# First MLP block: half-columns of 128 tokens for its first three columns, among the small products of chunk 1

## The chip, the cores and the metric

One core of a Trainium2 chip runs the program. TensorE (PE) multiplies, VectorE (DVE), ScalarE (ACT) and GpSimd (POOL) do the elementwise work, SyncE (SP) and ACT issue most DMAs. Each engine works through its own instructions in the order in which the program has them, and waits at semaphores for the others. The metric is the device time of one execution in microseconds, lower is better.

## The reference

A delta-rule attention over 768 steps, then two MLPs on its output, all in float32.

```python
# attention: q, k, v are (4, 8, 768, 48), beta is (4, 8, 768)
k_n = k / (norm(k) + 1e-06)
for t in range(S):
    y[:, :, t] = einsum('bhd,bhde->bhe', q[:, :, t], state)
    v_old = einsum('bhde,bhd->bhe', state, kt)
    state = state + bt * einsum('bhd,bhe->bhde', kt, vt - v_old)
x = y.transpose(0, 2, 1, 3).reshape(3072, 384)
# first MLP: d_ff 2048
h = x @ w_in
x = (maximum(h, 0) + alpha * minimum(h, 0)) @ w_out
# second MLP: d_ff 1536
g = x @ w_gate
out = (g * sigmoid(g) * (x @ w_val)) @ w_out2
```

## The kernel before

The 768 steps are cut into 24 chunks of 32; a chunk holds 4 batches x 32 steps = 128 tokens. Four chunks form a window. In a chunk c the recurrence is done with small products: KS (keys times state, `do_KS`, tile pk), QS (queries times state, py), U (the triangular inverse TT times v, tile pu), S (the state's update, pst), Y (py again, masked weights times U, copied to ys by ACT) and XT (PE transposes ys to px, ACT takes its rounded part as xh, DVE the rest as xl). Each small product is 32 matmuls, two instructions for each on PE. Chunk 0 has no state; for chunk 1, KS and QS are products with chunk 0's U, and S(1) does both chunks at once (128 instructions). The triangular inverse of a window comes from `lanes2` (window 0, with the products pi on PE) or `lanes` (the others: DVE and POOL eliminate row by row; it begins with two transposes into L on DVE and is called the solve below). `pre_T` (pt) transposes keys and queries of a window, `pre_G` (pg) makes their products, which ACT copies to GL and mt.

The first MLP works in blocks n of two chunks, 256 tokens, and 16 columns j of 128 hidden units. `H1(n, j)` is nine matmuls with 256 moving columns (three slices of 128 inputs, for each: high part times high, high times low, low times high), then ACT's Relu into pn and DVE's sum for the PReLU. `H1_parts` splits pn into gh: ACT rounds, POOL subtracts. `O1(n, j)` is nine matmuls more, whose last three need POOL's part; they add to the block's output in PSUM.

The weights of the first MLP arrive as 64-bit floats and are converted on the chip, one column at a time, by the generator `all_w1`, of which `go(conv)` does a step: three steps a column. The first has ACT's scaling of the next column's words, DVE's first pass, ACT's rounding of the column before (L887) and POOL's subtraction for it (L875, two halves); the second and third are DVE's second and third pass (L599, L603) and, from column 4 on, the loads of later columns, issued by ACT. Sixteen steps are in the prelude, the other 33 in the main loop's first eleven columns.

The order is written by hand. `prelude` (L913) is a straight list of calls. What follows it is a list of events, each with a due time in units of a column, sorted by it: H1(0, j) is due at j, its parts at j + 0.45, O1 at j + 2.5; chunk 2 and 3 get theirs from `base(c)`; the solve of window 1 has 37 steps between 10.9 and 22.6. The due times set only the order in which each engine gets its instructions.

The PSUM tiles of H1 rotate over two buffers, pn and gh over three each.

Of the kernel before, what the change touches and what calls it, by code (L numbers as in the profile page):

```python
# [24 lines left out]
def kernel(  # L25
# [646 lines left out]

    g1_t, o1_t = {}, {}

    def H1(n, j):
        ps = ps_h1.tile([128, 512], F32, name="h1", tag="h1")
        w = w1[j][:, 0]
        x = x1_t[n]
        i = 0
        for kk in range(NK):  # L680
            for a, b in PASSES:
                nc.tensor.matmul(  # L682
                    ps[:, 0:N1],
                    w[:, a, kk * 128:kk * 128 + 128],
                    x[b][:, kk, :],
                    start=(i == 0),
                    stop=(i == 3 * NK - 1),
                )
# [7 lines left out]
        g1_t[n, j] = g  # L696

    def H1_parts(n, j):
        g = g1_t[n, j]
        gh = g1.tile([128, 2, N1], F32R, name="gh", tag="gh", bufs=3)  # L700
# [313 lines left out]
    for w in range(1, NWIN):  # L1014
        P = base(4 * w) - 32
        if w == 1:
            for z in range(2):
                at(1.4 + 1.2 * z, lambda: go(inv0[0]))
            for z in range(4):
                at(1.8 + 1.05 * z, pre_T, 1, "q", z // 2, z % 2, nat)  # L1020
            for z in range(4):
                at((5.7, 7.0, 8.8, 10.4)[z], lambda z=z: pre_G(4 + z, raw=True))
                at(13.0 + 2 * z, mask_m, 4 + z)
            for z in range(2):
                at((4.3, 6.4)[z], lambda z=z: pre_G(2 + z, (1,), raw=True))
# [27 lines left out]
        for z in range(n):  # L1053
            at(l0 + (l1 - l0) * z / n, step)

    at(0.5, do_S, 1)
    at(0.6, load_k2, 2)
    for c in range(2, NCH):
        u = base(c)
        f = {2: 0.8, 3: 0.8, 4: 0.6, 5: 0.6}.get(c, 1.0)  # L1060
        if c > 2:
            at(u - 7, load_v, c)
            at(u - 1.3, load_k2, c)
        at(u - 1.5, scale_v, c)
        at(u + 0.3, do_KS, c)
        at(u + 0.35, do_QS, c)
        at(u + 0.3 + 2 * f, do_U, c)
        at(u + 0.3 + 4 * f, do_S, c)
        at(u + 0.3 + 5 * f, do_Y, c)
        at(u + 0.3 + (7 if c < 4 else 6) * f, do_XT, c)  # L1070
# [81 lines left out]
```

## Time and profile before

| | us |
|---|---|
| median of 3 runs | 1093.32 (1093.03 to 1093.74) |
| the profiled execution | 1094.43 |
| its span | 1092.5 |
| PE busy | 1055.2 (97%) |
| DVE busy | 603.6 (55%) |
| ACT busy | 389.9 (36%) |
| POOL busy | 359.5 (33%) |

The shares are means over very different stretches: the attention and the first MLP overlap in the first part, and the second MLP, almost all PE, fills the end. Times in the trace are counted from the span's start. A matmul's busy time includes the time it takes to run out behind the next one, so the distance from one start to the next is what a matmul costs in a row of them.

### The profile page before, as it was taken

The numbers are of one execution on the slowest core, as the hardware profiler recorded it, in microseconds if no ns is written. First come the engines' busy times: TensorE is split into PE (matmuls) and PEld (weight loads), VectorE is DVE, ScalarE is ACT, GpSimd is POOL, SyncE is SP. The second block draws the span as 40 slices with busy tenths as digits, with TensorE's granted clock in tenths as the row PEclk, the third lists the DMA queues.
The fourth block names the chain that finished last, engine by engine and source line by source line (L and its number), as shares of the span: only waits on it lengthen the run. The fifth ranks groups of instructions, "written<-read, shape, count | busy, mean of one in ns | idle before, by whom it ended". The sixth has DMA issues, their size and how long they took to land.

```text
span 1092.5 us, 35673 instructions
## 1 busy us (share of the span) xinstructions
PE 1055.2 (97%) x15649; PEld 969.6 (89%) x15649; DVE 603.6 (55%) x1204; ACT 389.9 (36%) x841; POOL 359.5 (33%) x531
## 2 busy tenths in 40 slices
PE   6689899999999999999999999999999999999998
PEld 5588788999999999999999998888888888888887
DVE  5778865975895697489453453433333333333332
ACT  3556343343434334433444653222222222222211
POOL 3478852832563383366333541101001001010000
PEclk9669999999999999999999999999999999999999
DMA  9663042353344236330441541010010010100001
GB/s 196 184 192 105 10 103 53 62 122 95 70 69 134 66 62 139 90 82 11 118 130 56 159 135 54 1 58 1 1 58 1 18 42 1 58 1 1 29 1 29
DMA packets 165979, 76.34 MB, mean 70 GB/s; under 512 B 129824, under 2 KB 160576, under 8 KB 165824
## 3 DMA queue, kind: packets, MB, share of 16 engines
q1 hardware_dynamic: 160256, 66.28, 24.5%
q10 hardware_dynamic: 5184, 7.37, 2.2%
q8 instruction: 122, 2.00, 0.8%
q0 software_dynamic: 384, 0.41, 0.2%
q14 instruction: 33, 0.27, 0.1%
HBM read 57.52 MB, written 16.52 MB: 68 GB/s over the span
## 4 chain that ended last, share of the span: by engine, by line
PE 89%; POOL 4%; issue 2%; DVE 2%; DMA 1%; ACT 1%; SPq 0%; ACTq 0%; POOLq 0%; DVEq 0%
PE gv L772 27%; PE o L713 18%; PE h L682 18%; PE o L802 14%; PE pst L527 2%; PE pg L207 2%; PE pu L506 2%; PE py L548 2%; PE pk L462 2%; PE py L462 1%; POOL w L875 1%; DMA nat<-in_k_dram 1%; POOL gh L702 1%; POOL X L331 1%; POOL tmg L323 1%
## 5 line engine op out<-in xcount | busy, mean ns | idle before, releaser
L772 PE MATMUL gv<-x2s,w 128*128 128x512 f32 x1296 | 307.6, 391 | 0.0
L772 PEld LDWEIGHTS gv<-x2s,w 128*128 128x128 f32 x1296 | 242.5, 188 | 47.8
L713 PE MATMUL o<-gh,w 128*128 128x256 f32 x1728 | 246.2, 288 | 3.9 <-POOL gh L702 3.9
L682 PE MATMUL h<-xh,w 128*128 128x256 f32 x1152 | 241.2, 286 | 3.0 <-DVE pn L693 1.6
L702 POOL TENSOR_TENSOR gh<-pn,gh 128x256 fp32r<-128x256 f32 x192 | 155.3, 809 | 248.5 <-ACT gh L701 217.3
L713 PEld LDWEIGHTS o<-gh,w 128*128 128x128 f32 x1728 | 217.3, 189 | 11.5 <-POOL gh L702 5.1
L682 PEld LDWEIGHTS h<-xh,w 128*128 128x128 f32 x1152 | 192.2, 191 | 5.8 <-DVE pn L693 2.6
L693 DVE SCALAR_TENSOR_TENSOR pn<-pn,slope,h 128x256 f32<-128x256 f32 x192 | 91.3, 476 | 135.9 <-ACT pn L692 135.9
L682 PE MATMUL h<-xl,w 128*128 128x256 f32 x576 | 163.2, 283 | 0.1
L802 PE MATMUL o<-w,us 128*128 128x384 f32 x864 | 162.5, 337 | 0.0
L802 PEld LDWEIGHTS o<-w,us 128*128 128x128 f32 x864 | 151.9, 188 | 7.1 <-DVE os L815 1.4
L692 ACT ACTIVATE pn<-h,slope 128x256 f32<-128x256 f32 x192 | 90.4, 471 | 137.7 <-PE h L682 134.5
L784 DVE TENSOR_TENSOR sg<-sg,gv 128x512 f32<-128x512 f32 x72 | 49.5, 687 | 151.8 <-ACT sg L782 151.7
L701 ACT ACTIVATE gh<-pn 128x256 fp32r<-128x256 f32 x192 | 80.0, 417 | 145.0 <-DVE pn L693 143.2
L682 PEld LDWEIGHTS h<-xl,w 128*128 128x128 f32 x576 | 109.8, 191 | 0.6 <-DVE xl L574 0.6
L757 POOL TENSOR_TENSOR x2s<-x2r,x2s 128x512 fp32r<-128x512 f32 x15 | 19.3, 1320 | 266.6 <-ACT x2s L755 266.6
L789 ACT ACTIVATE us<-u 128x512 fp32r<-128x512 f32 x72 | 45.5, 632 | 171.2 <-DVE u L785 171.2
L782 ACT ACTIVATE sg<-gv 128x512 f32<-128x512 f32 x72 | 43.0, 597 | 159.3 <-PE gv L772 159.3
L790 DVE TENSOR_TENSOR us<-u,us 128x512 fp32r<-128x512 f32 x72 | 49.9, 693 | 54.8 <-ACT us L789 54.8
L785 DVE TENSOR_TENSOR u<-sg,gv 128x512 f32<-128x512 f32 x72 | 49.5, 688 | 49.3 <-PE gv L772 48.8
L331 DVE TENSOR_TENSOR X<-X,tmp 128x31 f32<-128x31 f32 (+29 forms) x155 | 65.0, 419 | 4.8
L323 DVE TENSOR_TENSOR tmp<-L,X 128x31 f32<-128x31 f32 (+29 forms) x155 | 59.5, 384 | 1.8
(120 smaller groups left out, 975.9 us busy)
## 6 DMA issues: line engine op xcount, KB each, us to landing
w<-in_moe_w_out_dram SPq DMA_DIRECT2D x19, 384.0 KB
wf<-w2d SPq DMA_DIRECT2D x36, 192.0 KB
k<-in_k_dram SPq DMA_DIRECT2D x96, 48.0 KB
x2d<-xs SPq DMA_DIRECT2D x12, 384.0 KB
w<-in_moe_w_gate_dram SPq DMA_DIRECT2D x12, 384.0 KB
w<-in_moe_w_val_dram SPq DMA_DIRECT2D x12, 384.0 KB
x2r<-x2d SPq DMA_DIRECT2D x24, 192.0 KB
v<-in_v_dram SPq DMA_DIRECT2D x88, 48.0 KB
```

Source lines behind the costliest of these rows:

```text
L323: eng.tensor_tensor(w, t.L[:, i + 1:C, i:i + 1].to_broadcast([128, n, m]), t.X[:, i:i + 1, c0:c0 + m].to_broadcast([128, n, m]), ALU.mult,)
L331: eng.tensor_tensor(Xv, Xv, w, ALU.subtract)
L682: nc.tensor.matmul(ps[:, 0:N1], w[:, a, kk * 128:kk * 128 + 128], x[b][:, kk, :], start=(i == 0), stop=(i == 3 * NK - 1),)
L692: nc.scalar.activation(out=g, in_=hv, func=AF.Relu, scale=slope[:, 0, j:j + 1])
L693: nc.vector.scalar_tensor_tensor(out=g, in0=g, scalar=slope[:, 1, j:j + 1], in1=hv, op0=ALU.mult, op1=ALU.add)
L701: nc.scalar.activation(out=gh[:, 0], in_=g, func=AF.Copy)
L702: nc.gpsimd.tensor_tensor(gh[:, 1], g, gh[:, 0], ALU.subtract)
L713: nc.tensor.matmul(o[:, dm // 2, (dm % 2) * N1:(dm % 2) * N1 + N1], w[:, a, dm * 128:dm * 128 + 128], g[:, b], start=(j == 0 and i == 0 an ...
L772: nc.tensor.matmul(p[:, 0:N2], w2[j, z][:, a, kk * 128:kk * 128 + 128], x[:, b, kk], start=(i == 0), stop=(i == 3 * NK - 1),)
L784: nc.vector.tensor_tensor(sg, sg, ps[0], ALU.mult)
L790: nc.vector.tensor_tensor(us[:, 1], u, us[:, 0], ALU.subtract)
L802: nc.tensor.matmul(o2_t[n][t][:, 0:DM], us[:, a, t * 128:t * 128 + 128], w[:, b, :], start=(j == 0 and i == 0), stop=(j == J2 - 1 and i == 2),
```

## The change

In the prelude, chunk 0's QS and Y come before KS(1), and XT(0) right behind KS(1). Behind it QS(1), U(1) and Y(1) of chunk 1 follow, and between them and XT(1) stand the first halves (tokens 0 to 127, which are chunk 0's) of H1 and of the split for the columns 0, 1 and 2; the first half of O1 of column 0 closes the prelude. The second halves (tokens 128 to 255) of these three columns and their other halves of O1 are events of the main loop. H1, H1_parts and O1 get the token range as arguments; a half has nine matmuls as a whole has, with 128 moving columns.

The due times around the first eleven columns are other ones: S(1) goes from 0.5 to 2.6, KS and QS of a chunk no longer stand next to each other, and the pre_T, pre_G and mask events of window 1 and the last steps of window 0's inverse move.

```diff
-    def H1(n, j):
+    def H1(n, j, c0=0, c1=N1):
         ps = ps_h1.tile([128, 512], F32, name="h1", tag="h1")
...
+        hv = ps[:, c0:c1]
         for kk in range(NK):
             for a, b in PASSES:
                 nc.tensor.matmul(
-                    ps[:, 0:N1],
+                    hv,
                     w[:, a, kk * 128:kk * 128 + 128],
-                    x[b][:, kk, :],
+                    x[b][:, kk, c0:c1],
...
-    def O1(n, j):
-        if j == 0:
+    def O1(n, j, c0=0, c1=N1):
+        if j == 0 and c0 == 0:
...
-                    o[:, dm // 2, (dm % 2) * N1:(dm % 2) * N1 + N1],
+                    o[:, dm // 2, (dm % 2) * N1 + c0:(dm % 2) * N1 + c1],
                     w[:, a, dm * 128:dm * 128 + 128],
-                    g[:, b],
+                    g[:, b, c0:c1],
...
         do_U(0)
         go(conv, C_C)
-        do_KS(1)
         do_QS(0)
         do_Y(0)
+        do_KS(1)
         mark(nat[0][0:1, 0, 0, 0:1])
         load_nat(1, "q", nat)
         load_v(2)
         go(conv, 2)
-        do_U(1)
-        do_QS(1)
-        go(conv, 3)
         do_XT(0)
...
-        go(conv, C_D)
+        do_QS(1)
+        do_U(1)
+        go(conv, 1)
+        H1(0, 0, 0, 128)
+        go(conv, 1)
+        H1_parts(0, 0, 0, 128)
         do_Y(1)
         go(conv, 1)
+        H1(0, 1, 0, 128)
+        go(conv, C_D)
+        H1_parts(0, 1, 0, 128)
         do_XT(1)
+        go(conv, 1)
+        H1(0, 2, 0, 128)
+        H1_parts(0, 2, 0, 128)
+        O1(0, 0, 0, 128)
...
-        return {2: 2.9, 3: 7.7, 4: 22.6, 5: 27.2}.get(c, 8 * (c - 2))
+        return {2: 3.4, 3: 7.8, 4: 22.6, 5: 27.2}.get(c, 8 * (c - 2))
...
-                at((5.7, 7.0, 8.8, 10.4)[z], lambda z=z: pre_G(4 + z, raw=True))
+                at(6.6 + z, lambda z=z: pre_G(4 + z, raw=True))
...
+    FIRST = {2: (3.6, 4.6, 5.1, 6.1, 7.1, 8.15), 3: (8.1, 9.1, 10.1, 11.1, 12.1, 12.8)}
+    at(2.6, do_S, 1)
+    at(2.7, load_k2, 2)
...
     for n in range(NB1):
         for j in range(J1):
+            if n == 0 and j < 3:
+                at(0.7 * j, H1, n, j, 128, N1)
+                at(0.7 * j + 0.3, H1_parts, n, j, 128, N1)
+                if j > 0:
+                    at(0.7 * j, O1, n, j, 0, 128)
+                at(2.1 + 0.01 * j if j < 1 else 2.5 + j, O1, n, j, 128, N1)
+                continue
```

On PE, from U(0) to the first column of the MLP, before (pu is U, pk is KS, py is QS or Y, px is XT, h is H1; mx and mt are the weights of the products with chunk 0's U and of the masked ones):

```order
L506 MATMUL pu<-v,TT 32x48 x32
L475 MATMUL pk<-U,mx 32x48 x32
L548 MATMUL py<-U,mt 32x48 x32
L506 MATMUL pu<-v,TT 32x48 x32
L475 MATMUL py<-U,mx 32x48 x32
L570 MATMUL px<-ident,ys 128x128 x3
L548 MATMUL py<-U,mt 32x48 x32
L570 MATMUL px<-ident,ys 128x128 x3
L682 MATMUL h_1025<-xh,w 128x256
```

and of the change, from the same U(0), where h_965 is the first half of column 0:

```order
L506 MATMUL pu<-v,TT 32x48 x32
L548 MATMUL py<-U,mt 32x48 x32
L475 MATMUL pk<-U,mx 32x48 x32
L570 MATMUL px<-ident,ys 128x128 x3
L475 MATMUL py<-U,mx 32x48 x32
L506 MATMUL pu<-v,TT 32x48 x32
L683 MATMUL h_965<-xh,w 128x128
L683 MATMUL h_965<-xl,w 128x128
L683 MATMUL h_965<-xh,w 128x128 x2
L683 MATMUL h_965<-xl,w 128x128
L683 MATMUL h_965<-xh,w 128x128 x2
L683 MATMUL h_965<-xl,w 128x128
```

Chunk 0's transposes (px) stand two products earlier, and the nine matmuls of a half-column follow chunk 1's U; behind them come Y(1), nine more of column 1, XT(1), and nine more of column 2.

On POOL, in the same place and the main loop's first columns, before (w is a converted weight's low part, two instructions, named by its words w_113 of column 3 and so on; gh is a column's split, v the scaling of a chunk's v):

```order
L875 TENSOR_TENSOR w<-w_113,w 128x384 x2
L875 TENSOR_TENSOR w<-w_114,w 128x384 x2
L875 TENSOR_TENSOR w<-w_115,w 128x384 x2
L702 TENSOR_TENSOR gh<-pn,gh 128x256
L875 TENSOR_TENSOR w<-w_116,w 128x384 x2
L452 TENSOR_TENSOR v<-v,nn 128x384
L702 TENSOR_TENSOR gh<-pn,gh 128x256
L875 TENSOR_TENSOR w<-w_117,w 128x384 x2
L702 TENSOR_TENSOR gh<-pn,gh 128x256
```

and of the change:

```order
L883 TENSOR_TENSOR w<-w_113,w 128x384 x2
L707 TENSOR_TENSOR gh<-pn,gh 128x128 x2
L883 TENSOR_TENSOR w<-w_114,w 128x384 x2
L707 TENSOR_TENSOR gh<-pn,gh 128x128
L883 TENSOR_TENSOR w<-w_115,w 128x384 x2
L707 TENSOR_TENSOR gh<-pn,gh 128x128 x2
L883 TENSOR_TENSOR w<-w_116,w 128x384 x2
L707 TENSOR_TENSOR gh<-pn,gh 128x128
L452 TENSOR_TENSOR v<-v,nn 128x384
L883 TENSOR_TENSOR w<-w_117,w 128x384 x2
```

Two of the split's halves now stand ahead of the weights of column 4, three ahead of those of column 5, and all six ahead of those of column 7, where before one whole split stood ahead of column 6's.

On PE, about column 7 of the main loop, before (o is O1, pk and py here are KS and QS of chunk 3):

```order
L548 MATMUL py<-U,mt 32x48 x32
L713 MATMUL o_1253<-gh,w 128x256 x9
L462 MATMUL pk<-St,kqt 32x48 x32
L682 MATMUL h_1880<-xh,w 128x256
L682 MATMUL h_1880<-xl,w 128x256
L682 MATMUL h_1880<-xh,w 128x256 x2
L682 MATMUL h_1880<-xl,w 128x256
L682 MATMUL h_1880<-xh,w 128x256 x2
L682 MATMUL h_1880<-xl,w 128x256
L682 MATMUL h_1880<-xh,w 128x256
L462 MATMUL py<-St,kqt 32x48 x32
L713 MATMUL o_1253<-gh,w 128x256 x9
```

and of the change, from the same Y(2):

```order
L548 MATMUL py<-U,mt 32x48 x32
L721 MATMUL o_1069<-gh,w 128x256 x9
L207 MATMUL pg<-kqt 32x64 x32
L683 MATMUL h_1879<-xh,w 128x256
L683 MATMUL h_1879<-xl,w 128x256
L683 MATMUL h_1879<-xh,w 128x256 x2
L683 MATMUL h_1879<-xl,w 128x256
L683 MATMUL h_1879<-xh,w 128x256 x2
L683 MATMUL h_1879<-xl,w 128x256
L683 MATMUL h_1879<-xh,w 128x256
L462 MATMUL pk<-St,kqt 32x48 x32
L570 MATMUL px<-ident,ys 128x128 x3
```

Chunk 3's KS stands a column's H1 later there, with a pre_G in its place, and its QS a further column later.

## Rows read from the trace of the kernel before

**Rows 1.** Busy time by stretch: us, then each engine, clock, DMA share, GB/s.

```profile
40.00:50.00 10.00, 6.56 (x299) 5.69 (x291) 6.98 (x8) 6.18 (x10) 3.85 (x4) 0.59 0.44 109
...
130.00:140.00 10.00, 6.85 (x53) 6.02 (x51) 9.42 (x20) 3.15 (x9) 9.14 (x19) 1.00 0.08 30
...
160.00:180.00 20.00, 20.00 (x614) 18.44 (x607) 8.45 (x19) 7.62 (x20) 4.93 (x6) 1.00 0.26 72
```

**Rows 2.** Waits of PE, 36 to 150 us: total, times, longest.

```profile
PE o L713 <- POOL gh L702: 3.9, 6, 1.8
PE py L548 <- issue: 2.0, 1, 2.0
...
PE pk L462 <- issue: 2.0, 1, 2.0
...
PE pg L207 <- issue: 1.2, 1, 1.2
```

**Rows 3.** Timeline of PE before column 0: start, length, operation, wait before.

```profile
51.76 1.01 PE L548 MATMUL py<-U,mt 32*32 32x48 f32 x36 [2.00 <-issue]
53.41 0.90 PE L570 MATMUL px<-ident,ys 128*128 128x128 f32 x3 [0.64 <-ACT ys L557]
55.68 0.58 PE L682 MATMUL h<-xh,w 128*128 128x256 f32 x1 [1.37 <-ACT xh L573]
```

**Rows 4.** Busy time in stretches of 2 us; the clock is third from last.

```profile
50.00:52.00 2.00, 0.24 (x13) 0.24 (x16) 1.37 (x3) 0.57 (x2) 2.00 (x3) 0.91 1.15 259
...
66.00:68.00 2.00, 2.00 (x10) 2.00 (x11) 1.93 (x4) 2.00 (x6) 0.65 (x1) 0.50 0.88 244
...
70.00:72.00 2.00, 2.00 (x136) 1.97 (x136) 1.97 (x2) 1.81 (x4) 2.00 (x3) 1.00 0.82 243
...
76.00:78.00 2.00, 2.00 (x67) 1.88 (x58) 1.88 (x2) 0.00 (x0) 2.00 (x3) 0.50 1.09 341
```

**Rows 5.** Chain of waits, 0 to 200 us: start, length, what.

```profile
58.35 3.60 PE pst L527 x128
61.95 2.22 PE h L682 x9
...
79.77 1.06 PE h L682 x9
```

**Rows 6.** Weight loads of PE by shape: busy us, mean ns.

```profile
L682 PEld LDWEIGHTS h<-xh,w 128*128 128x128 f32 x1152 | 192.2, 191 | 5.8 <-DVE pn L693 2.6 <-ACT xh L573 1.8
...
L527 PEld LDWEIGHTS pst<-U,k 32*64 32x64 f32 x1472 | 25.0, 140 | 2.9 <-issue 0.4
L506 PEld LDWEIGHTS pu<-v,TT 32*32 32x32 f32 x1536 | 19.3, 109 | 4.4 <-issue 0.8 <-POOL w L875 0.7
```

**Rows 7.** Timeline of PE in the second MLP, with 512 moving columns.

```profile
904.58 4.29 PE L772 MATMUL gv<-x2s,w 128*128 128x512 f32 x18
908.71 2.25 PE L802 MATMUL o<-w,us 128*128 128x384 f32 x12
```

**Rows 8.** Timeline of DVE, chunk 1's xl to the solve's first transpose.

```profile
55.66 0.56 DVE L574 TENSOR_TENSOR xl<-px,xh 128x384 fp32r<-128x384 f32 x1 [0.88 <-ACT xh L573]
...
57.20 1.66 DVE L603 SCALAR_TENSOR_TENSOR w<-w 128x768 int32<-128x768 int32 x1
...
62.01 0.56 DVE L540 COPY St<-pst 128x384 f32<-128x384 f32 x1 [1.16 <-PE pst L527]
...
65.64 0.48 DVE L693 SCALAR_TENSOR_TENSOR pn<-pn,slope,h 128x256 f32<-128x256 f32 x1 [2.12 <-ACT pn L692]
...
73.46 0.47 DVE L693 SCALAR_TENSOR_TENSOR pn<-pn,slope,h 128x256 f32<-128x256 f32 x1
...
112.87 1.11 DVE L269 STREAM_TRANSPOSE L<-GL 128x512 f32<-128x512 f32 x1 [1.74 <-ACT GL L217]
```

**Rows 9.** Waits of DVE, 50 to 150 us.

```profile
DVE pn L693 <- ACT pn L692: 6.2, 6, 2.1
DVE xl L574 <- ACT xh L573: 3.2, 3, 1.7
```

More of the change, by code (lines that the diff above doesn't have):

```diff
@@ L689, in H1 @@
                 i += 1
-        hv = ps[:, 0:N1]
-        g = g1.tile([128, N1], F32, name="pn", tag="pn", bufs=3)
+        if c0 == 0:
+            g1_t[n, j] = g1.tile([128, N1], F32, name="pn", tag="pn", bufs=3)
+        g = g1_t[n, j][:, c0:c1]
         nc.scalar.activation(out=g, in_=hv, func=AF.Relu, scale=slope[:, 0, j:j + 1])
@@ L695, in H1, with H1_parts @@
         )
[L696 to L700, printed above, removed]
+    gh_t = {}
+    def H1_parts(n, j, c0=0, c1=N1):
+        g = g1_t[n, j][:, c0:c1]
+        if c0 == 0:
+            gh_t[n, j] = g1.tile([128, 2, N1], F32R, name="gh", tag="gh", bufs=3)
+        gh = gh_t[n, j][:, :, c0:c1]
         nc.scalar.activation(out=gh[:, 0], in_=g, func=AF.Copy)
         nc.gpsimd.tensor_tensor(gh[:, 1], g, gh[:, 0], ALU.subtract)
-        g1_t[n, j] = gh
-    def O1(n, j):
-        if j == 0:
+        if c1 == N1:
+            g1_t.pop((n, j))
+    def O1(n, j, c0=0, c1=N1):
+        if j == 0 and c0 == 0:
             o1_t[n] = ps_o1.tile([128, 2, 512], F32, name="o1", tag="o1")
@@ L709, in O1 @@
         w = w1[j][:, 1]
-        g = g1_t.pop((n, j))
+        g = gh_t[n, j]
+        if c1 == N1:
+            gh_t.pop((n, j))
         for i, (a, b) in enumerate(((0, 0), (1, 0), (0, 1))):
@@ L713, in O1 @@
                 nc.tensor.matmul(
-                    o[:, dm // 2, (dm % 2) * N1:(dm % 2) * N1 + N1],
+                    o[:, dm // 2, (dm % 2) * N1 + c0:(dm % 2) * N1 + c1],
                     w[:, a, dm * 128:dm * 128 + 128],
-                    g[:, b],
-                    start=(j == 0 and i == 0 and dm % 2 == 0),
+                    g[:, b, c0:c1],
+                    start=(j == 0 and i == 0 and dm % 2 == 0 and c0 == 0),
                     stop=(j == J1 - 1 and i == 2),
@@ L1017 @@
             for z in range(2):
-                at(1.4 + 1.2 * z, lambda: go(inv0[0]))
+                at(3.1 + z, lambda: go(inv0[0]))
             for z in range(4):
-                at(1.8 + 1.05 * z, pre_T, 1, "q", z // 2, z % 2, nat)
+                at((3.7, 4.7, 5.15, 5.65)[z], pre_T, 1, "q", z // 2, z % 2, nat)
             for z in range(4):
-                at((5.7, 7.0, 8.8, 10.4)[z], lambda z=z: pre_G(4 + z, raw=True))
+                at(6.6 + z, lambda z=z: pre_G(4 + z, raw=True))
                 at(13.0 + 2 * z, mask_m, 4 + z)
             for z in range(2):
-                at((4.3, 6.4)[z], lambda z=z: pre_G(2 + z, (1,), raw=True))
-                at((4.9, 7.5)[z], mask_m, 2 + z)
+                at((5.6, 10.6)[z], lambda z=z: pre_G(2 + z, (1,), raw=True))
+                at((6.3, 11.2)[z], mask_m, 2 + z)
             l0, l1, n = 10.9, 22.6, LANES
@@ L1054 @@
             at(l0 + (l1 - l0) * z / n, step)
-    at(0.5, do_S, 1)
-    at(0.6, load_k2, 2)
+    FIRST = {2: (3.6, 4.6, 5.1, 6.1, 7.1, 8.15), 3: (8.1, 9.1, 10.1, 11.1, 12.1, 12.8)}
+    at(2.6, do_S, 1)
+    at(2.7, load_k2, 2)
     for c in range(2, NCH):
         u = base(c)
-        f = {2: 0.8, 3: 0.8, 4: 0.6, 5: 0.6}.get(c, 1.0)
+        f = {4: 0.6, 5: 0.6}.get(c, 1.0)
         if c > 2:
@@ L1064 @@
         at(u - 1.5, scale_v, c)
[L1065 to L1070, printed above, removed]
+        cols = [u + 0.3 + z * f for z in (0, 0.05, 2, 4, 5, 6)]
+        for x, fn in zip(FIRST.get(c, cols), (do_KS, do_QS, do_U, do_S, do_Y, do_XT)):
+            at(x, fn, c)
     for n in range(NB1):
         for j in range(J1):
+            if n == 0 and j < 3:
[5 more added lines that the diff above has]
+                continue
             at(16 * n + j, H1, n, j)
```

## The prediction

> **What bounds the kernel now.** I read the busy share by stretch first, then the waits of TensorE (PE), then PE's own timeline where it waits, then the clock, and last the engine that is late next.
>
> The stretches [rows 1] show three regimes. From 160 us PE is busy 20.00 of 20 us: what comes later is a fixed quantity of matmuls, and whatever is won or lost before moves the end by the same amount. Between 40 and 50 us PE is busy 6.56 of 10 us, because chunk 1's small products hang on each other. Between 130 and 140 us it is busy 6.85 of 10 while VectorE (DVE) has 9.42 and GpSimd (POOL) 9.14: there the triangular solve of window 1 sets the pace. The change works before that stage and on the way to it.
>
> From 36 to 150 us PE's waits [rows 2] are of two kinds. Waits for "issue" (the largest 2.0, 2.0 and 1.2 us) are stops in which no engine is late; waits for POOL's gh (3.9 us) belong to the solve. Between 56 and 112 us PE waits for no other engine, so its own work is the bound there, while ScalarE (ACT), DVE and POOL convert the weights in the same rhythm, interleaved with the columns in program order.
>
> The timeline of PE before the first MLP column [rows 3] shows the holes: 2.00 us in the middle of chunk 1's last product, 0.64 us before its transposes, 1.37 us before column 0. The granted clock [rows 4] is 0.91 at 50 to 52 us, 0.50 from 52 us, still 0.50 at 66 to 68 us, and 1.00 at 70 to 72 us; there is a second fall, 0.50 at 76 to 78 us, behind the 2.0 us stop in KS. At 0.50 (1.2 GHz) the nine matmuls of a column's first product take 2.22 us, at 1.00 (2.4 GHz) 1.06 us [rows 5].
>
> **The change part by part.** The sum is made at one place, the start of the solve of window 1 (its L transposes, 112.87 us [rows 8]), against the profiled execution of 1094.43 us (span 1092.5 us and 1.9 us around it). That one is 1.1 us above the median of 1093.32 us.
>
> Order of chunk 0 and 1 before the MLP. Product Y(0) now stands before KS(1), and XT(0) before U(1). U(1) becomes later by the length of Y(0) less what it waited for; Y(1) then ends near 53.0 us as before (52.8 us, [rows 3]), because the 2.00 us stop comes at a place counted in instructions and shrinks as the work before it gets longer. I take 0 for this reordering, with -1 and +1.5 us as ends (half the stop gained, or one half-column of 9 matmuls at the low clock between Y(1) and XT(1) lying on the chain). On the queues of ACT and DVE the same sixteen conversion steps are issued in this part; SP's loads keep their order except that v of chunk 3 now goes ahead of k of chunk 2, both long before their use, which I cost at nothing: PE has some ten columns' work to cover them.
>
> More matmuls. Three columns of 18 matmuls with 256 moving columns become six half-columns of 18 with 128. Behind chunk 1's transposes PE has 54 such matmuls before; now 90 of the half size (36 of H1 and 54 of O1; of these 18 before the main loop, the rest in it). The price of a half-size one isn't in the trace. Low end: from 512 columns (18 in 4.13 us, 229 ns each [rows 7]) to 256 (1.06/9 = 118 ns [rows 5]) a matmul loses 0.43 ns per column, which makes 62 ns for 128. High end: 118 ns, no saving at all, because each of them still needs its own 128 weight columns loaded: the loads take 109, 140 and 191 ns for 32, 64 and 128 columns [rows 6], 0.85 ns per column or 109 ns for the 128, about what 256 moving columns take. A load can hide behind one matmul before it, and behind 128 columns only half of it fits. I take 118 ns: 36 x 0.118 = +4.2 us. The low end gives 90 x 0.062 - 54 x 0.118 = -0.8 us; at 2.22/9 = 247 ns (low clock) it is +8.9 us.
>
> The Trainium skill, "TensorE: Matmul & The Clock Gate", section "LDWEIGHTS (loading the stationary operand)", says that a load's time is its columns over 1.2 in ns, whatever the rows: 107 ns for 128. This speaks against halving, and the slope of the three load rows agrees with it. By that rule the term would be 90 x 0.107 - 6.4 = +3.3 us. The same page, "Back-to-back issue gap", gives about 81 ns for 128 columns sustained, by which it would be +0.9 us; no run here shows it yet.
>
> Clock. Before, PE ran at 0.50 from about 55.7 to 68.7 us, 13 us for work that takes 6.2 at 1.00: 6.8 us. What preceded the fall was the 2.00 us stop and the holes behind it. Now nine matmuls stand before Y(1), nine between Y(1) and XT(1), nine behind it, so that PE hardly stops between 48 us (when the clock had risen) and the main loop. I take it that the clock stays up: -6.8 us; ends 0 and -8.6 us (with the second fall, 3.5 us x 0.52 = 1.8 us, of which I take half, -0.9).
>
> Stops for issue behind 56 us. 2.0 and 1.2 us [rows 2] come where groups of 64 small matmuls are adjacent (KS next to QS, pg next to S and pg). The new order puts one group between the 9 matmuls of H1 and those of O1 in more places. The number of instructions isn't lower, so I take half: -1.6 us of 3.2 (ends 0 and -3.2).
>
> PE alone: 4.2 - 6.8 - 0.9 - 1.6 = -5.1 us.
>
> **What is late next.** DVE. From the end of chunk 1's xl (55.66 + 0.56 us) to column 3's pn at 73.46 us [rows 8] it has 17.2 us, of which 1.16 + 2.12 = 3.3 us are waits; in that stretch it then has four half-size pn instead of three whole ones (0.47 us each), which I count as 0.5 us more. So column 3 can come 2.8 us earlier at most, however fast PE is. The rest must come in the columns 4 to 10, where DVE waits too: all its waits for PE by way of ACT sum to 6.2 + 3.2 + 1.7 us [rows 8, 9], so the far end for the whole stage is -11 us. The last GL now comes from pre_G at 9.6 instead of 10.4, which takes away DVE's 1.74 us wait at 112.87 us. Of the 2.3 us left of PE's gain I believe half, 1.2 us: -4.0 us in all. The solve stage and all behind it are shifted whole, since POOL and DVE (solve) and then PE (to the end) have the same work. 1094.43 - 4.0 = 1090.4 us for a profiled execution, 1089.3 us as a median.
>
> **Rivals.**
> 1. Halves at the low clock (slower). If the clock falls all the same at 52 us and stays at 0.50 as it did before, the nine groups behind Y(1) (H1 of columns 1 and 2, O1 of 0, three second H1, two first O1 halves and the second of column 0) take 1.92 us each by the full price (2.22 less 0.3 us, the end of the last matmul, which the next group covers). From 53.0 us this reaches 71 us, and S(1) (3.60 us for its 128 small matmuls [rows 5]) 74.6 us. Before, column 3 had its pn at 73.46 us, some 2 us behind the start of its H1, so it begins 3 us later; the pi products and transposes that were done by then are still to come (+2), less 2 us of stops: +3 us, 1096.3 us. It decides from the point where column 3 begins after 73.5 us. For it: from 56 to 68 us PE worked without a hole and stayed at 0.50. Against: the holes ahead of the fall are shorter.
> 2. The conversion hides it. ACT, DVE and POOL go through the weights one per column in either kernel, and of these DVE's third pass alone takes 1.66 us at 57.20 us [rows 8]. If DVE holds 5.2 us per column, PE's gain turns into waits for pn: within 1.5 us of before, 1092.5 us.
> 3. The halves are cheap (62 ns), the clock stays up and the stops go: -0.8 - 8.6 - 3.2 = -12.6 us for PE, cut by DVE to about -8: 1085.3 us.
>
> **How the numbers follow.** Main case 0.42 (1087.5 to 1091.3 us); rival 1 0.17; rival 2 0.25; rival 3 0.16. Faster or slower by 0.2% means 2.2 us, about what a measurement of this kernel tells from no change. Faster: 0.39 + 0.03 + 0.16 = 0.58; slower: 0.15 + 0.01 = 0.16; same: 0.26. The range leaves out half of rival 3's far side and half of rival 1's: 1084.8 to 1095.8 us.
>
> **What would show it.** Right: granted clock 1.00 from 54 to 70 us; column 3's pn between 70 and 72 us; L transposes near 109 us; 9 half-size matmuls in about 1.0 us. Wrong: clock 0.50 in that stretch and column 3 after 73.5 us (rival 1); DVE without waits and PE waiting for pn, L transposes near 112 us (rival 2); 9 halves in under 0.7 us (rival 3).

## The result: slower by 1.1%, and the profile after

| | before | after |
|---|---|---|
| median of 6 runs each, same chip, us | 1094.21 (1093.03 to 1096.12) | 1105.88 (1101.99 to 1109.58) |
| ratio, 95% interval | | 1.0107 [1.0085, 1.0128] |
| profiled execution: span, mean granted clock | 1092.5, 0.984 | 1104.0, 0.966 |

The forecast was 1089.3 us, between 1084.8 and 1095.8, with a chance of 0.16 for slower. The change costs 11.7 us, and the range does not hold it.

The stretches that answer to [rows 1] (us; busy time of PE, PEld, DVE, ACT, POOL; clock, DMA share, GB/s):

```profile
40.00:50.00 10.00, 7.93 (x318) 6.92 (x309) 5.98 (x9) 4.93 (x9) 4.69 (x4) 0.55 0.57 136
130.00:140.00 10.00, 8.79 (x71) 8.25 (x70) 9.62 (x29) 2.68 (x7) 9.06 (x21) 1.00 0.12 22
160.00:180.00 20.00, 19.48 (x549) 18.33 (x537) 9.47 (x22) 9.36 (x26) 5.79 (x8) 1.00 0.30 78
```

PE's holes from 40 to 50 us did shrink (7.93 of 10 us busy, before 6.56). From 160 to 180 us PE is full but for 0.52 us (19.48, before 20.00). Most of the loss lies between.

The clock comes next. These are stretches of 2 us of the changed kernel, with the same columns, as in [rows 4].

```profile
54.00:56.00 2.00, 2.00 (x21) 1.88 (x11) 0.00 (x0) 0.49 (x1) 1.58 (x3) 0.50 0.44 83
...
66.00:68.00 2.00, 2.00 (x11) 2.00 (x11) 1.94 (x2) 1.59 (x2) 2.00 (x2) 0.50 0.79 239
70.00:72.00 2.00, 2.00 (x11) 2.00 (x10) 1.97 (x2) 0.68 (x1) 2.00 (x2) 0.50 0.94 320
...
76.00:78.00 2.00, 2.00 (x9) 1.81 (x9) 1.37 (x2) 0.49 (x1) 0.24 (x1) 0.50 0.69 160
84.00:86.00 2.00, 2.00 (x11) 2.00 (x10) 1.61 (x2) 0.66 (x2) 0.80 (x2) 0.50 0.31 40
```

The clock falls in the same place as before, but where it was back at 70 to 72 us [rows 4] it is now at 0.50 in every stretch up to 86 us, although PE is full in each of them. The trace also records when the granted clock changes. By these records the low stretches behind 50 us are 52.5 to 86.6 and 90.1 to 93.5 us; before they were 51.7 to 68.7 and 75.5 to 79.0: 20.5 us have become 37.5.

PE's timeline there (start, length, operation, wait before) shows the halves:

```profile
50.73 0.44 PE L548 MATMUL py<-U,mt 32*32 32x48 f32 x19
53.09 1.18 PE L548 MATMUL py<-U,mt 32*32 32x48 f32 x45 [1.93 <-issue]
54.20 0.48 PE L683 MATMUL h<-xh,w 128*128 128x128 f32 x1
...
58.65 2.12 PE L721 MATMUL o<-gh,w 128*128 128x128 f32 x9
60.57 0.41 PE L683 MATMUL h<-xh,w 128*128 128x128 f32 x1
...
72.22 3.67 PE L527 MATMUL pst<-U,k 32*64 32x48 f32 x128
75.82 0.58 PE L683 MATMUL h<-xh,w 128*128 128x256 f32 x1
...
84.18 0.56 PE L683 MATMUL h<-xh,w 128*128 128x256 f32 x1
```

Nine half-size matmuls of O1 take from 58.65 to 60.57 us, 0.213 us each. The long row of half-size matmuls ends at 72.22 us, where S(1) begins, and column 3's H1, of whole size, starts at 75.82 us. So the clock stays low through half-size matmuls first, and then through S(1), columns 3 and 4, nine more halves of O1 and the small products between them.

The stop in Y(1) is still there, 1.93 us against 2.00 [rows 3], but at another place in it: behind the 19th of its 64 matmul instructions, where before it stood behind the 28th:

```profile
49.23 0.53 PE L548 MATMUL py<-U,mt 32*32 32x48 f32 x28
```

The nine half-size matmuls that now stand ahead of Y(1) have moved it forward by nine. Counted along PE's matmul instructions such stops come at fixed distances. Before, 128 and 127 matmuls lie between the stops that end at 43.69, 47.07 and 51.76 us, and 511 more up to the one at 75.32 us; in the change 255 lie between those at 44.01 and 53.09 us, and 638 more up to the one at 90.11 us. Each is a multiple of 128, less two at most; not every multiple shows a stop.

The waits of PE from 36 to 150 us (total, times, longest), to be held against [rows 2]:

```profile
PE py L548 <- issue: 3.3, 2, 1.9
PE o L721 <- POOL gh L707: 2.9, 2, 1.8
PE pi L430 <- issue: 2.3, 1, 2.3
PE py L548 <- POOL mt L195: 1.9, 1, 1.9
PE py L462 <- issue: 0.8, 1, 0.8
```

Of the kernel before, this view also has two stops that stand before 44 us:

```profile
PE pk L475 <- issue: 2.0, 1, 2.0
...
PE pi L430 <- issue: 2.0, 1, 2.0
```

In all, the waits for issue sum to 10.8 us before and to 6.4 us now; behind 56 us they sum to 4.2 us (2.0, 1.2, 0.6 and 0.4) and to 0.8 us. So they have become fewer. One wait is new: Y(2) for its mask on POOL, 1.9 us.

DVE's timeline, as in [rows 8], and its waits from 50 to 150 us, as in [rows 9]:

```profile
78.71 0.48 DVE L695 SCALAR_TENSOR_TENSOR pn<-pn,slope,h 128x256 f32<-128x256 f32 x1 [1.34 <-ACT pn L694]
...
120.14 1.12 DVE L269 STREAM_TRANSPOSE L<-GL 128x512 f32<-128x512 f32 x1
123.46 0.48 DVE L695 SCALAR_TENSOR_TENSOR pn<-pn,slope,h 128x256 f32<-128x256 f32 x1 [2.20 <-ACT pn L694]
...
124.89 1.13 DVE L269 STREAM_TRANSPOSE L<-GL 128x512 f32<-128x512 f32 x1
```

```profile
DVE pn L695 <- ACT pn L694: 16.5, 10, 3.5
```

Column 3's pn is 5.25 us late (78.71 against 73.46) and the first L transpose 7.27 us (120.14 against 112.87). DVE waits 16.5 us for pn by way of ACT, before 6.2. The wait for GL is gone, but between the two transposes DVE now waits 2.20 us for a column's pn. The second transpose is therefore 9.67 us late; before it stood here:

```profile
115.22 1.08 DVE L269 STREAM_TRANSPOSE L<-GL 128x512 f32<-128x512 f32 x1
```

The end is 11.5 us late. The rest is lost about 182 us, where PE has a stop for issue of 1.95 us (up to 181.43 us), and behind it the clock is low from 182.2 to 185.6 us (a stretch of 4 us):

```profile
182.00:186.00 4.00, 4.00 (x77) 3.60 (x76) 0.64 (x2) 1.05 (x3) 0.00 (x0) 0.57 0.01 4
```

A column's pn ahead of it is 9.48 us late (176.40 against 166.92 us), one behind it 11.76 us (205.52 against 193.76). Another short low stretch, from 144.7 to 148.1 us, falls into the solve and costs at most 0.4 us: the pn on either side are 9.17 and 9.49 us late (137.75 against 128.58, 152.80 against 143.31). The kernel before has neither low stretch.

### The profile page after: what moved, and what is told of

It is laid out like the page before. It is cut to its first block, busy times and chain, and to the rows that moved or that the text cites. A ratio compares the mean times of both kernels' runs of the same rounds, so it can differ in the third digit from the quotient of the medians.

```text
span 1104.0 us, 35796 instructions
## 1 busy us (share of the span) xinstructions
PE 1070.3 (97%) x15703; PEld 986.3 (89%) x15703; DVE 604.1 (55%) x1207; ACT 391.9 (36%) x847; POOL 358.1 (32%) x534
## 4 chain that ended last, share of the span: by engine, by line
PE 91%; POOL 3%; issue 2%; DMA 2%; DVE 1%; SPq 1%; ACT 0%; ACTq 0%; POOLq 0%; DVEq 0%
PE gv L780 27%; PE o L721 19%; PE h L683 19%; PE o L810 13%; PE pst L527 2%; PE pg L207 2%; PE py L548 2%; PE pu L506 2%; PE pk L462 2%; PE py L462 2%; PE px L570 1%; PE pt L185 1%; POOL tmg L323 1%; POOL X L331 1%; POOL gh L707 1%
## 5 line engine op out<-in xcount | busy, mean ns | idle before, releaser
L721 PE MATMUL o<-gh,w 128*128 128x256 f32 (+1 forms) x1755 | 253.4, 291 | 3.7 <-POOL gh L707 3.6
L683 PE MATMUL h<-xh,w 128*128 128x256 f32 (+1 forms) x1170 | 249.7, 290 | 0.5 <-DVE pn L695 0.5
L707 POOL TENSOR_TENSOR gh<-pn,gh 128x256 fp32r<-128x256 f32 (+1 forms) x195 | 156.8, 804 | 252.7 <-ACT gh L706 225.9
L721 PEld LDWEIGHTS o<-gh,w 128*128 128x128 f32 x1755 | 224.4, 192 | 9.9 <-POOL gh L707 4.9
L683 PEld LDWEIGHTS h<-xh,w 128*128 128x128 f32 x1170 | 199.8, 195 | 2.6 <-DVE pn L695 0.9
L695 DVE SCALAR_TENSOR_TENSOR pn<-pn,slope,h 128x256 f32<-128x256 f32 (+1 forms) x195 | 91.8, 471 | 148.8 <-ACT pn L694 148.8
L683 PE MATMUL h<-xl,w 128*128 128x256 f32 (+1 forms) x585 | 168.1, 287 | 0.1
L694 ACT ACTIVATE pn<-h,slope 128x256 f32<-128x256 f32 (+1 forms) x195 | 91.0, 467 | 145.0 <-PE h L683 142.8
L706 ACT ACTIVATE gh<-pn 128x256 fp32r<-128x256 f32 (+1 forms) x195 | 80.5, 413 | 143.0 <-DVE pn L695 141.4
L683 PEld LDWEIGHTS h<-xl,w 128*128 128x128 f32 x585 | 114.3, 195 | 0.3 <-DVE xl L574 0.3
```

Source lines behind the costliest of these rows:

```text
L683: nc.tensor.matmul(hv, w[:, a, kk * 128:kk * 128 + 128], x[b][:, kk, c0:c1], start=(i == 0), stop=(i == 3 * NK - 1),)
L695: nc.vector.scalar_tensor_tensor(out=g, in0=g, scalar=slope[:, 1, j:j + 1], in1=hv, op0=ALU.mult, op1=ALU.add)
L721: nc.tensor.matmul(o[:, dm // 2, (dm % 2) * N1 + c0:(dm % 2) * N1 + c1], w[:, a, dm * 128:dm * 128 + 128], g[:, b, c0:c1], start=(j == 0 a ...
```

## The experiments

Theories at the start: the halves cost time because the clock stays low under them (and each costs what a whole costs); the new due times cost time by waits of their own. Every ratio is to the kernel before, timed along with the run.

**The two parts apart.** First the change without its halves: new prelude order, new due times, whole columns.

```diff
-        H1(0, 0, 0, 128)
-        H1_parts(0, 0, 0, 128)
...
-            if n == 0 and j < 3:
-                at(0.7 * j, H1, n, j, 128, N1)
...
-                continue
```

> The change without its halves: the new order of chunks 0 and 1 and the new due times stay, columns 0 to 2 are whole and stand at their old due times. Theory P (the halves cost what wholes cost, 0.112 us a matmul at 2.4 GHz and 0.213 us at 1.2 GHz, and the clock stays low under them): the loss goes, 1090 to 1096 us, and the clock is back at 1.00 before 72 us. Rival O (the new order and due times make the loss): 1102 us or more, with column 3's pn late (after 77 us) all the same.

Measured: 1098.02 us, ratio 1.0039 [1.0024, 1.0054], between the two expected ranges. The clock is back at 60.8 us, but low again from 67.6 to 71.0 and from 77.8 to 88.1 us. PE's waits, its timeline, and POOL's timeline:

```profile
PE o L721 <- POOL gh L707: 6.3, 5, 2.5
PE py L548 <- issue: 4.9, 2, 2.5
...
PE py L548 <- POOL mt L195: 2.0, 1, 2.0
```

```profile
65.97 0.62 PE L721 MATMUL o<-gh,w 128*128 128x256 f32 x3 [2.53 <-POOL gh L707]
66.52 2.80 PE L527 MATMUL pst<-U,k 32*64 32x48 f32 x128
```

```profile
62.18 2.73 POOL L883 TENSOR_TENSOR w<-w,w 128x384 fp32r<-128x384 f32 x2 [1.36 <-ACT w L895]
64.88 1.03 POOL L707 TENSOR_TENSOR gh<-pn,gh 128x256 fp32r<-128x256 f32 x1
```

So the new order and due times alone cost some 4 us. With S(1) moved behind O1(0,0), PE has nothing to do while POOL finishes a weight and the split; before, S(1) filled that time.

Whether these waits or the clock are the price of the due times was asked with unread matmuls in this kernel's holes:

```diff
+        fill(16)
...
+        fill(4)
...
+        fill(7)
```

> The new order with whole columns, and unread matmuls in its holes: 16 ahead of Y(1), 4 ahead of XT(1), 7 behind it. If the order loses its 4 us by the clock alone: 1092 to 1094 us. If it loses them by waits that it makes itself (O1 of column 0 for POOL with S(1) now behind it, Y(2) for its mask): those 4.5 us stay in the trace and the time is 1095 to 1098 us.

Measured: 1097.29 us, 1.0035 [1.0019, 1.0051], with a mean clock of 0.980 over the timed executions (0.975 without the fills). The clock is better and the time is not, and O1's waits for gh (6.3 us in all) are still in its trace. This speaks for waiting as the price. It does not prove it: the same kind of fill in the kernel before also gives a better clock and no better time (below).

Second, the halves alone: before's order and due times, the first three columns in two halves back to back.

```diff
-            at(16 * n + j, H1, n, j)
+            for c in ((0, 128), (128, N1)) if n == 0 and j < 3 else ((0, N1),):
+                at(16 * n + j, H1, n, j, *c)
```

> The kernel before with only the halving: columns 0 to 2 are done in two halves back to back at the place of the whole, order and due times as before. Theory P: 54 matmuls more on a PE that is the bound there, at 0.112 to 0.213 us each, +6 to +11.5 us, 1100 to 1106 us, and the clock stays at 0.50 for longer than to 68.7 us. Rival O: the halving is paid by at most 1 to 2 us, 1094 to 1097 us.

Measured: 1105.59 us, 1.0109 [1.0094, 1.0124], within theory P's range and as much as the whole change; the clock is low from 53.3 to 84.1 us. The parts are not a sum: 4 and 12 us apart, 11.7 together. Here all 54 additional matmuls stand behind chunk 1's transposes, in the change 36.

**The price of a half by itself.** Block 6's H1, far from the start and at full clock, in two halves for all 16 columns: 144 matmuls more.

```diff
+        for c0, c1 in ((0, 128), (128, N1)) if n == 6 else ((0, N1),):
+            i = 0
```

> The kernel before; in block 6 alone (where PE is the bound and the clock 1.00) H1 of all 16 columns is done in two halves of 128 moving columns: 144 matmuls more. Theory P (a half costs its load of 128 weight columns, 0.109 to 0.112 us): 288 x 0.111 - 144 x 0.118 = +15 us. Rival N (a half costs its 128 moving columns, 0.062 us): +1 us.

Measured: 1108.37 against 1093.34 us, 1.0137 [1.0119, 1.0155], +15.0 us. In its timeline of PE the nine starts lie 0.11 us apart:

```profile
430.63 0.28 PE L684 MATMUL h<-xl,w 128*128 128x128 f32 x1
...
430.97 0.27 PE L684 MATMUL h<-xl,w 128*128 128x128 f32 x1
431.08 0.39 PE L684 MATMUL h<-xh,w 128*128 128x128 f32 x2
```

Four matmuls from 430.63 to 431.08 are 0.112 us each, against 0.118 for 256 columns [rows 5]. 288 x 0.111 - 144 x 0.118 = 15.0. Half the columns save 6% of the time: the split nearly doubles the cost (288 matmuls of 0.111 us for 144 of 0.118). The Trainium skill, "TensorE: Matmul & The Clock Gate", section "LDWEIGHTS (loading the stationary operand)", puts a load of 128 columns at 107 ns; the 0.112 us here lies close to it. The 81 ns that the Trainium skill, same page, section "Back-to-back issue gap", has for 128 moving columns was not reached here.

**The stop.** Twelve unread matmuls of 384 columns ahead of Y(1), in the changed kernel:

```diff
+        fill(12)
         do_Y(1)
```

> The changed kernel with 12 matmuls of 384 columns whose result nobody reads, in the place of the stop ahead of Y(1) (1.9 us of PE at 2.4 GHz). Theory S (the stop of 1.9 us lets the clock fall at 52.5 us, and the 34 us at 0.50 are its consequence): the clock is 1.00 from 52 to 70 us, Y(1) ends at most 1 us later, the time falls by 8 to 14 us to 1092 to 1098 us. Rival H (the clock falls or stays low under the half-size matmuls whatever stands before them): 0.50 again within some us of 54 us, 1104 to 1108 us.

Measured: 1097.43 us, 1.0038 [1.0024, 1.0052]; some 7.5 of the 11.7 us come back. Its timeline has no stop in Y(1), and the halves behind it run at full speed; its stretches show a later fall:

```profile
51.47 2.33 PE L880 MATMUL warm<-w 128*128 128x384 f32 x12
53.73 0.88 PE L548 MATMUL py<-U,mt 32*32 32x48 f32 x64
54.54 0.33 PE L683 MATMUL h<-xh,w 128*128 128x128 f32 x1
...
56.91 1.17 PE L721 MATMUL o<-gh,w 128*128 128x128 f32 x9
57.91 0.28 PE L683 MATMUL h<-xh,w 128*128 128x128 f32 x1
```

```profile
56.00:58.00 2.00, 2.00 (x21) 2.00 (x20) 1.80 (x4) 1.58 (x5) 1.03 (x2) 1.00 0.80 230
...
62.00:64.00 2.00, 1.19 (x10) 1.19 (x10) 1.97 (x4) 1.38 (x3) 1.27 (x2) 0.95 0.76 264
64.00:66.00 2.00, 2.00 (x11) 2.00 (x11) 2.00 (x4) 1.17 (x3) 2.00 (x2) 0.50 0.82 275
...
74.00:76.00 2.00, 2.00 (x136) 1.81 (x135) 1.54 (x4) 0.98 (x3) 2.00 (x2) 0.99 0.90 248
```

Nine of O1 take 1.0 us (56.91 to 57.91) instead of 1.92. So with the stop filled the fall at 52.5 us does not come, and the time is within theory S's range. The clock falls all the same later, at 63.8 us, behind holes of PE of 0.49 and 1.02 us (waits for pn), and is back at 74 us. What is left of the loss, 1.0038, is what the order and the due times cost without any halves (1.0039).

The same fill in the kernel before, in its three holes:

```diff
+        fill(12)
...
+        fill(4)
...
+        fill(7)
```

> The kernel before with such unread matmuls in its three holes: 12 ahead of Y(1), 4 ahead of XT(1), 7 ahead of column 0. Theory S: the clock stays at 1.00 from 48 us, the 13 us at 0.50 go, -4 to -7 us, 1087 to 1090 us. Rival H' (the fall has another cause than the holes): 0.50 from about 52 us all the same, and the fillers cost 0 to +3 us, 1094 to 1097 us.

Measured: 1093.11 us, 0.9999 [0.9984, 1.0013]. The clock stays at 1.00 from 52.1 to 69.2 us, then it is low until 79.4 us, behind a stop of 1.22 us. So the low clock behind 52 us is halved (10.2 us, before 20.5), and the mean clock over all timed executions is better too (0.983 against 0.980), but the time is the same and misses theory S's range. Column 0 starts 1.7 us later (57.36 against 55.68 us), and column 3's pn is no earlier (73.88 against 73.46 us). In the kernel before, a better clock alone won no time.

**Size or number.** The halves in the old place, but with every matmul over all 256 columns, so that number and order are the same.

```diff
-                    hv,
+                    ps[:, wide],
...
-                    x[b][:, kk, c0:c1],
+                    x[b][:, kk, wide],
```

> Before's order and due times with the columns 0 to 2 in two halves back to back, as in the experiment of that name, but each half's nine matmuls of H1 and of O1 go over all 256 columns (both halves are computed whole, so that the first three columns are added to block 0's output twice: its output is changed in that). The number of matmuls and of weight loads and the order are those of the halves in the old place (1105.6 us). Theory H (it is the half-size matmuls, whose time is the weight load, that keep the clock at 0.50 for 34 us; the number of matmuls alone costs 54 x 0.118 = 6 us or less at 1.00): the clock is back at 1.00 near 70 us as in before, the L transposes stand near 117 to 119 us, 1098 to 1101 us. Rival N (the number of matmuls ahead of the small products and the stops that they bring keep it low, whatever their size): 0.50 until 80 us or later, L transposes at 122 us or more, 1105 us or more.

Stretches of the halves alone, then of this kernel:

```profile
60.00:62.00 2.00, 2.00 (x88) 2.00 (x82) 1.89 (x4) 1.73 (x4) 0.59 (x1) 0.50 0.16 25
...
76.00:78.00 2.00, 2.00 (x11) 2.00 (x11) 0.92 (x1) 1.08 (x3) 1.23 (x2) 0.50 0.57 143
```

```profile
56.00:58.00 2.00, 2.00 (x11) 2.00 (x11) 1.97 (x2) 0.37 (x1) 1.29 (x1) 0.50 0.78 249
60.00:62.00 2.00, 2.00 (x119) 1.95 (x114) 1.76 (x4) 1.94 (x4) 0.38 (x1) 0.92 0.19 26
...
76.00:78.00 2.00, 2.00 (x83) 1.97 (x71) 1.35 (x2) 0.67 (x2) 2.00 (x3) 1.00 0.87 252
```

In both kernels the clock falls at the same time (53.3 and 53.5 us) and PE then has eighteen matmuls of 0.213 us each, half-size or whole. With whole-size ones the clock is back by 60.3 us, and low once more from 67.2 to 70.6 us, behind a hole of 2.52 us; with half-size ones it is not back until 84.1 us. The mean granted clock of all timed executions says the same: 0.976 here (0.972 to 0.980), 0.968 with halves (0.966 to 0.969), 0.979 before. So the clock follows the size, as theory H has it.

The time does not: 1104.05 us, 1.0093 [1.0072, 1.0115], where it expected 1098 to 1101, and the halves' 1.0109 [1.0094, 1.0124] can't be told from it. The trace is of the shortest of six executions (1098.64 us, first L transpose at 117.44 us, within H's bounds) and does not show where the others lost 5 us more. A sum for the median comes near: of 10.1 us over before, 0.003 x 1092 = 3.3 us of lost clock and 54 x 0.118 = 6.4 us of more matmuls are 9.7. But the same sum for the halves, 0.011 x 1092 + 54 x 0.111 = 18.0 us, is far above the 11.6 measured, so it proves little. In this place the number of matmuls may carry as much of the loss as the clock; that is open.

**Which half, which due time.** The change with O1 of columns 0 to 2 whole:

```diff
-        O1(0, 0, 0, 128)
...
-                if j > 0:
-                    at(0.7 * j, O1, n, j, 0, 128)
-                at(2.1 + 0.01 * j if j < 1 else 2.5 + j, O1, n, j, 128, N1)
+                at(2.1 if j < 1 else 2.5 + j, O1, n, j)
```

> The changed kernel with O1 of the columns 0 to 2 whole, at its old place; the halves of H1 stay. 27 matmuls fewer than the change. Theory P: 27 x 0.11 to 0.21 us less, 3 to 6 us, 1100 to 1103 us. Rival K (the halves of H1 between the small products are what hurts, by delaying chunk 1): no more than 1 us less, 1104 to 1106 us.

Measured: 1098.65 us, 1.0047 [1.0028, 1.0065]. It is below both expected ranges. In its trace the clock is low from 53.2 to 80.5 us even so, but over half of the loss is gone, and what is left is near what the order and the due times cost (1.0039). So O1's halves carry more of it than H1's. Whether they do it by their number (27 x 0.111 to 0.213 us are 3.0 to 5.8 us) or by the clock (0.976 over all timed executions, in the change 0.968) is not told apart.

The prelude's order alone:

```diff
-        do_KS(1)
         do_QS(0)
         do_Y(0)
+        do_KS(1)
```

> The kernel before with only the new order of chunks 0 and 1 ahead of the main loop (whole columns, old due times). Prediction's term: 0 with -1 and +1.5 us as ends, 1092.5 to 1095 us. Rival O: the loss of the order lies here, 1097 us or more.

Measured: 1093.6 us, 1.0010 [0.9997, 1.0024]: no difference. So the 4 us of order and due times lie in the due times of the main loop. With the first half of H1 of column 0 ahead of Y(1) in addition:

```diff
+        H1(0, 0, 0, 128)
+        H1_parts(0, 0, 0, 128)
```

> The run above with one half-column alone: column 0's first half of H1 ahead of Y(1), its second half in the main loop, O1 whole. Nine matmuls more, nine of them in a hole of PE. Theory P: the second half costs the whole's price, so nothing is won behind XT(1) and nothing lost: within 1 us of the run above. If halves cost 0.062 us: 1 us faster than it. If they hold the clock down: 3 us or more slower.

Measured: 1093.64 us, 1.0006 [0.9994, 1.0019]. One half placed in a hole is free, and wins nothing.

Of the due times, first S(1) and chunk 2's masked product and mask back, whole columns:

```diff
-    at(2.6, do_S, 1)
+    at(0.5, do_S, 1)
```

> The new order with whole columns, but S(1) and chunk 2's masked product and mask at their old due times (0.5, 4.3, 4.9). If the order's loss is its own waits: PE no longer waits 2.5 us for POOL in O1 of column 0 nor 2.0 us for the mask in Y(2), and the time is within 1.5 us of the kernel before, 1092.5 to 1095.5 us. If it is anything else: 1097 to 1099 us as with the whole order.

Measured: 1096.31 us, 1.0023 [1.0013, 1.0034]. Both waits, O1's of 2.5 us and Y(2)'s for its mask, are gone, and the time lies between the two expected ranges. The gain over the whole order (1.0039) is not clear of the noise. Then chunk 3's masked product and mask back too:

```diff
-                at((4.9, 11.2)[z], mask_m, 2 + z)
+                at((4.9, 7.5)[z], mask_m, 2 + z)
```

> As the run before with S(1) and chunk 2's mask at their old due times, and chunk 3's masked product and mask also back (6.4 and 7.5), so that before column 11's H1 stands one small product, not two. Theory W (the rest of the order's loss is DVE's 2.20 us wait for column 11's pn between the two L transposes): that wait goes, the transposes are 2.4 us apart as before, and the time is 1093 to 1095 us. Otherwise: 1096 us as in that run.

Measured: 1095.81 us, 1.0030 [1.0016, 1.0045]: nothing more. DVE's wait between the two L transposes shrank from 2.19 to 1.16 us and did not go; they stand 3.65 us apart, in the run before 4.76. The time did not follow, so theory W is not borne out, though not fully tried either. From there, either the steps of window 0's inverse and the pre_T went back, or those of chunks 2 and 3:

```diff
-                at(3.1 + z, lambda: go(inv0[0]))
+                at(1.4 + 1.2 * z, lambda: go(inv0[0]))
```

> The change's order with whole columns and S(1), the masked products and masks of chunks 2 and 3 at the old due times (1095.8 us), and now also window 0's last inverse steps (1.4, 2.6, 3.8, 5.0) and the four pre_T of window 1 at the old ones; only the base and the steps of KS, QS, U, Y, S of chunks 2 and 3 stay new. Theory T (the inverse and the transposes, moved behind columns 3 to 5, hold the rest of the loss): 1093 to 1094 us. Theory C (the chunks' steps hold it): 1095.5 to 1096.5 us, as without this edit. If both share it, 1094.5 to 1095.2 us.

```diff
-        return {2: 3.4, 3: 7.8, 4: 22.6, 5: 27.2}.get(c, 8 * (c - 2))
+        return {2: 2.9, 3: 7.7, 4: 22.6, 5: 27.2}.get(c, 8 * (c - 2))
```

> The same starting point (1095.8 us), and now the steps KS, QS, U, Y, S of chunks 2 and 3 back at their old distances and bases; window 0's inverse steps and the pre_T stay at the new due times. Theory C (the chunks' steps hold the rest of the loss): 1093 to 1094 us. Theory T: 1095.5 to 1096.5 us.

Measured: 1093.36 us, 0.9999 [0.9987, 1.0010], with inverse and pre_T back; 1099.66 us, 1.0063 [1.0046, 1.0080], with the chunks back. The first is theory T; the second lies 3 us above what theory T expected. PE's timeline has the inverse's first product, of the starting point and then with the step put back:

```profile
69.04 1.26 PE L408 MATMUL pi<-TT,GL 32*32 32x16 f32 x128 [2.22 <-DVE pn L695]
```

```profile
64.09 1.58 PE L408 MATMUL pi<-TT,GL 32*32 32x16 f32 x128
```

The tile pi comes from the two rotating PSUM buffers of H1 (`bank`, with `early` set). At the new due time the product stands behind a further column, and waits 2.22 us until DVE has read a column out of the buffer that it needs; at the old one it has no wait and stands 5 us earlier. The clock moves with it: behind this wait it is low from 70.3 to 84.0 us, with the step put back it is at 1.00 from 62.1 to 86.0 us. So the due times of the inverse and the pre_T together are shown to cost the rest, but not how much of that is wait and how much clock. With the chunks at their old due times and the inverse late, PE's waits have larger stops for issue:

```profile
PE pk L462 <- issue: 3.9, 2, 3.5
```

It is worse by 3.6 us than with both late; whether these stops are the cause was not tried. The version with the inverse put back has stops of 6.0 us in Y and is as fast as the kernel before, so stops alone don't tell.

The due times of S(1) and of both chunks' masked products and masks put back in the change with its halves:

```diff
-    at(2.6, do_S, 1)
+    at(0.5, do_S, 1)
```

> The changed kernel, halves and all, with these three due times back. If the order's waits and the price of the halves add up: 3 to 4 us less than the change, 1101 to 1103 us, of which 8 are the halves. If PE's surplus of half-size matmuls hides the order's waits: 1105 to 1106 us as the change.

Measured: 1107.99 us, 1.0130 [1.0106, 1.0154], no better, and above both expectations. Both waits are gone from its trace, and its clock is low from 55.5 to 96.4 us. With the halves in, taking the waits away wins nothing; that the low clock is why is a reading of this one trace.

**A version to beat both.** Three first halves of H1, the twelve unread matmuls, O1 whole, old due times:

```diff
+        H1(0, 0, 0, 128)
...
+        fill(12)
...
+            c = (128, N1) if n == 0 and j < 3 else (0, N1)
+            at(16 * n + j, H1, n, j, *c)
```

> A candidate to beat both: the change's prelude with the first halves of H1 of columns 0 to 2, twelve unread matmuls of 384 columns ahead of Y(1), O1 in wholes, and all due times of the main loop as before. Theory G (with the stop filled the clock stays up, and halves at 1.00 cost 27 x 0.111 = 3 us of PE time that stands in the holes of chunk 1): clock 1.00 from 50 us on, L transposes at 109 to 111 us, 1090 to 1093 us. Rival (the half-size matmuls bring the clock down again as with the fill in the change, 63.8 to 74.0 us there): a stretch of 0.50 of about 10 us, L transposes at 113 us or later, 1095 us or more.

Measured: 1096.49 us, 1.0026 [1.0013, 1.0039]: the rival's side. The clock is low again, from 63.1 to 73.4 us in the trace's clock records, as with the fill in the change. The profiled execution took 1092.69 us, the shortest of twelve, and its first L transpose, at 111.27 us, is earlier than the rival had it. No version here beats the kernel before.

## Why the prediction was wrong

- **What bounds the kernel:** right in the main. PE was the bound up to the solve, and what was lost there came to the end whole. It was not only shifted, though: 2.4 us more came between the L transposes and 2.3 us about 182 us (7.3 at the first transpose, 11.5 at the end). And PE's holes from 40 to 50 us were read wrongly: of 3.4 us, 2.6 are stops for issue (1.99 and 0.60 us) and only 0.60 is a wait for another engine.
- **Order of chunk 0 and 1, taken as 0:** right by itself (1.0010). With the halves in it, Y(1) ended at 54.3 us instead of 53.0, and chunk 1's transposes began 2.8 us later than before (56.18 against 53.41), because nine half-size matmuls at the low clock stood ahead of them; the far end of the term had this at 1.5.
- **Due times of the main loop:** no term in the sum, save a gain for GL. They cost about 4 us, by steps that now stand behind work that has to wait. For the inverse behind a column, together with the pre_T, some 3 us of this are shown (1.0030 and 0.9999); for S(1) behind O1(0,0) and Y(2) behind its mask the waits are in the trace, but their price is within the noise.
- **Price of a half-size matmul, 118 ns:** right, 111 at full clock. But 81 of the 90 behind chunk 1's transposes were paid at 213.
- **Clock, "I take it that the clock stays up":** the step that failed. It rested on the 2.00 us stop becoming shorter; the stop stayed at 1.93 us, the clock fell at 52.5 us, and the low stretches grew from 20.5 to 37.5 us. With the stop filled 7.5 us of the 11.7 came back. Nothing in the sum asked whether the clock would come back under half-size matmuls: it did not before 86.6 us, 14 us after the row of them had ended. The terms of -6.8 and -0.9 us became a loss. Nor is it shown that they could have been won: in the kernel before, with its stops filled, the low clock was halved and the time stayed. That is rival 2's outcome; whether it came by rival 2's way, the conversion on DVE, was not tried.
- **Stops, -1.6 us:** the sign was right and the size too small. Behind 56 us the waits for issue went from 4.2 to 0.8 us, near the far end of -3.2. That PE won no time by it fits its low clock there; it was not tried.
- **DVE late next, 4.0 us left:** not reached. PE was late, and DVE waited 16.5 us for it.
- **Rival 1** had the mechanism: it ended the nine groups at 71 us and S(1) at 74.6 us; measured 72.22 and 75.82. It was too small for what follows, since it ended the low clock there, and for the due times. Its 0.17 was too little: the trace of before already showed the clock at 0.50 through 12 us in which PE had no hole, and this spoke for it.

## What to carry to other kernels

Where each matmul loads its own 128 weight columns, cutting the moving columns from 256 to 128 nearly doubles PE's time for them, and a gain from filling holes must beat that. The stops for issue seen here keep their place in the count of PE's matmuls: nine matmuls put ahead moved one by nine and left its length. So count before forecasting that such a stop goes, and if a term rests on the clock behind it, first try unread matmuls in its place, in the kernel before too: there they bettered the clock and won nothing. A step that moves behind a column takes over what that column waits for: read the waits of what it is now queued behind.

## What the runs showed of the hardware

- At 2.4 GHz a matmul with 128 x 128 weights took 0.111 us with 128 moving columns and 0.118 with 256; at 1.2 GHz both took 0.213.
- Stops for issue of 0.6 to 2.3 us, with no engine late, came after 127, 128, 255, 511 or 638 matmuls: multiples of 128, less two at most. One of them went when twelve unread matmuls of 384 columns were put ahead of it.
- A PE without a hole stayed at 1.2 GHz from 54 to 86 us, with half-size matmuls up to 72 us and whole-size and small ones behind them; in the kernel before, with whole-size and small ones, from 56 to 68 us. At the same place and in the same number, whole-size matmuls had the clock back at 60.3 us and half-size ones at 84.1 us (one trace of each; the mean clock over all executions was 0.976 and 0.968).
- After one fill of the stop the fall came later, not never: at 63.8 us in the change, at 69.2 us in the kernel before, each for about 10 us.
